# Attention decode with 32 heads: query projection, output projection and FFN weights moved into the head loop

## The chip, the cores and the metric

The kernel runs on one core of one Trainium2 chip. The metric is device time in microseconds (us) of one execution, as the median over several runs. The core has five engines with a queue each (PE for matmuls, DVE for vector work, ACT for activations and copies, POOL, and SP), and 16 DMA engines that all DMA queues feed. SP and ACT issue DMAs on a hardware queue each; POOL can issue DMAs too, which the kernel before does not do.

## The reference

One token goes through one transformer layer: a layer norm, attention of 32 heads over a cache of 32768 keys, a residual, a second layer norm, and a two-layer FFN with ReLU and a residual.

```
x: [1,1,640]   k_cache, v_cache: [1,32,32768,192]   wq: [640,6144]   wo: [6144,640]   w1: [640,1536]   w2: [1536,640]   (all bf16)

q  = (layernorm(x) @ wq) as 32 heads of 192
p  = softmax(q . k * 192**-0.5)           per head, over 32768 keys
o  = p . v                                per head
h  = x + concat(o) @ wo
out = h + relu(layernorm(h) @ w1) @ w2
```

The two caches are 805 MB together and are read once; all weights together are 20 MB.

## The kernel before

It has three stages.

**Start.** `x` is loaded and normalised on one partition. Ten short matmuls spread the result over 128 partitions (`LB`, line 95). The whole of `wq` comes in one DMA on SP's queue (line 97); 160 matmuls of 128x192 (line 101) make each head's query, already spread over all partitions, and 32 copies (line 103) leave them in `QB`.

**Head loop.** 32 heads of 8 chunks of 4096 keys, 256 chunks in all. For each chunk a K tile (SP's queue, line 120) and a V tile (ACT's queue, line 125) of 1536 KB each are loaded; both pools have three buffers. A tile holds 32 keys on each partition. For each of the 32, DVE multiplies 128x192 keys by the query and sums along the row into one column of the score tile `S` (line 133). Each such instruction shows in the trace as a pair: the product (`CUSTOM_DVE_ANT_0`) and a read of the accumulator into `S` (`DVE_READ_ACCUMULATOR2_ANT`). There are 8192 pairs. `S` is bf16 (line 14 and 129). ACT takes the exponential of `S` into `E` and its row sum into `ZP` (line 138); PE multiplies `E` with the V tile, 32 matmuls a chunk, summed in PSUM over the head (line 141); ACT copies the head's sum out (line 145).

**End.** The softmax sums are reduced and inverted (lines 151 to 155), each head's output is scaled and turned onto partitions by 64 products (lines 159 and 161), `wo` is loaded as `WOA` and `WOB` (lines 170 and 171), and 128 matmuls project it (lines 175 and 177, 64 of 512 columns, 64 of 128). Then come the residual (line 181), the second layer norm (lines 186 to 204), `W1` and `W2` (loaded on lines 212 and 214), and the FFN (lines 207 to 239).

The program's text sets the order of work only in part: the framework's scheduler places the instructions on each engine by their dependences and buffers, and adds the waits. Each engine takes its own list in order.

Of the kernel before, what the change touches and what calls it, by code (L numbers as in the profile page):

```python
# [7 lines left out]
F32 = mybir.dt.float32  # L8
BF16 = mybir.dt.bfloat16
ACT = mybir.ActivationFunctionType  # L10
ALU = mybir.AluOpType
AX = mybir.AxisListType

SCORE_BF16 = True


@with_exitstack
def kernel(
# [12 lines left out]
    nc = tc.nc  # L31
    P = nc.NUM_PARTITIONS

    _, _, D = A_x.shape
    _, H, Sk, Dh = A_k_cache.shape
    HD = H * Dh
    Dff = B_w1.shape[1]
    DC = D // P
    FC = Dff // P
    inv_sqrt_dh = Dh ** -0.5  # L40
    eps = 1e-5
    P64 = Dh - P

    CH = 4096 if Sk % 4096 == 0 else Sk
    assert Sk % CH == 0
    J = CH // P
    CN = Sk // CH

    persist = ctx.enter_context(tc.tile_pool(name="persist", bufs=1))
    ones11 = persist.tile([1, 1], F32)  # L50
# [3 lines left out]
    ones_col = persist.tile([P, 1], F32)  # L54
    nc.vector.memset(ones_col[:], 1.0)
    x32 = persist.tile([1, D], F32)
    QB = persist.tile([P, H, Dh], BF16)
    OUTR = persist.tile([1, H, Dh], F32)
    ZP = persist.tile([P, H, CN], F32)

    with (
        tc.tile_pool(name="pro_sb", bufs=1) as psb,
        tc.tile_pool(name="pro_sb2", bufs=2) as psb2,
        tc.tile_pool(name="pro_ps", bufs=1, space=bass.MemoryType.PSUM) as pps,
        tc.tile_pool(name="pro_ps2", bufs=2, space=bass.MemoryType.PSUM) as pps2,
    ):
        xbf = psb.tile([1, D], BF16)
        nc.sync.dma_start(out=xbf[:], in_=A_x[0])
        nc.vector.tensor_copy(out=x32[:], in_=xbf[:])
        msum = psb.tile([1, 1], F32)  # L70
        nc.vector.reduce_sum(out=msum[:], in_=x32[:], axis=AX.X)
        negmean = psb.tile([1, 1], F32)
        nc.vector.tensor_scalar_mul(out=negmean[:], in0=msum[:], scalar1=-1.0 / D)
        cen = psb.tile([1, D], F32)
        nc.vector.tensor_scalar_add(out=cen[:], in0=x32[:], scalar1=negmean[:, 0:1])
        junk_r = psb.tile([1, D], F32)
        var = psb.tile([1, 1], F32)
        nc.vector.tensor_tensor_reduce(
            out=junk_r[:], in0=cen[:], in1=cen[:], scale=1.0 / D, scalar=0.0,
            op0=ALU.mult, op1=ALU.add, accum_out=var[:],  # L80
        )
        vareps = psb.tile([1, 1], F32)
        nc.vector.tensor_scalar_add(out=vareps[:], in0=var[:], scalar1=eps)
        std = psb.tile([1, 1], F32)
        nc.scalar.activation(std[:], vareps[:], ACT.Sqrt)
        rstd = psb.tile([1, 1], F32)
        nc.vector.reciprocal(out=rstd[:], in_=std[:])
        ln32 = psb.tile([1, D], F32)
        nc.vector.tensor_scalar_mul(out=ln32[:], in0=cen[:], scalar1=rstd[:, 0:1])
        LB_ps = pps.tile([P, DC, P], F32)  # L90
        for c in range(DC):
            nc.tensor.matmul(LB_ps[:, c, :], lhsT=ln32[0:1, c * P:(c + 1) * P], rhs=ones_row[0:1, :],
                             start=True, stop=True)
        LB = psb.tile([P, DC, P], BF16)
        nc.vector.tensor_copy(out=LB[:], in_=LB_ps[:])
        WQ = psb.tile([P, DC, HD], BF16)
        nc.sync.dma_start(out=WQ[:], in_=A_wq.rearrange("(c p) n -> p c n", p=P))
        for h in range(H):
            qb_ps = pps2.tile([P, Dh], F32)
            for c in range(DC):  # L100
                nc.tensor.matmul(qb_ps[:], lhsT=LB[:, c, :], rhs=WQ[:, c, h * Dh:(h + 1) * Dh],  # L101
                                 start=(c == 0), stop=(c == DC - 1))
            nc.any.tensor_copy(out=QB[:, h, :], in_=qb_ps[:])  # L103

    k_h = A_k_cache[0]
    v_h = A_v_cache[0]

    with (
        tc.tile_pool(name="kpool", bufs=3) as kpool,
        tc.tile_pool(name="vpool", bufs=3) as vpool,  # L110
        tc.tile_pool(name="spool", bufs=2) as spool,
        tc.tile_pool(name="epool", bufs=2) as epool,
        tc.tile_pool(name="jpool", bufs=2) as jpool,
        tc.tile_pool(name="opsum", bufs=2, space=bass.MemoryType.PSUM) as opsum,
    ):
        for h in range(H):
            o_ps = opsum.tile([1, Dh], F32)
            for c in range(CN):
                Kt = kpool.tile([P, J, Dh], BF16)
                nc.sync.dma_start(  # L120
                    out=Kt[:],
                    in_=k_h[h, c * CH:(c + 1) * CH, :].rearrange("(p j) d -> p j d", p=P),
# [3 lines left out]
                    out=Vt[:],  # L126
                    in_=v_h[h, c * CH:(c + 1) * CH, :].rearrange("(p j) d -> p j d", p=P),
                )
                S = spool.tile([P, J], BF16 if SCORE_BF16 else F32)
                with nc.allow_low_precision(reason="scores tiny; bf16 accum enables DVE 2x mode"):  # L130
                    for j in range(J):
                        junk = jpool.tile([P, Dh], BF16)
                        nc.vector.tensor_tensor_reduce(  # L133
                            out=junk[:], in0=Kt[:, j, :], in1=QB[:, h, :], scale=inv_sqrt_dh,
                            scalar=0.0, op0=ALU.mult, op1=ALU.add, accum_out=S[:, j:j + 1],
                        )
                E = epool.tile([P, J], BF16)
                nc.scalar.activation(E[:], S[:], ACT.Exp, bias=0.0, scale=1.0,  # L138
                                     accum_out=ZP[:, h, c:c + 1])
                for j in range(J):  # L140
                    nc.tensor.matmul(  # L141
                        o_ps[0:1, :], lhsT=E[:, j:j + 1], rhs=Vt[:, j, :],
                        start=(c == 0 and j == 0), stop=(c == CN - 1 and j == J - 1),
                    )
            nc.scalar.copy(out=OUTR[0:1, h, :], in_=o_ps[0:1, :])  # L145

    esb = ctx.enter_context(tc.tile_pool(name="epi_sb", bufs=1))
    nblk = [(0, 0, 512), (1, 512, D - 512)]
    with tc.tile_pool(name="eps1", bufs=1, space=bass.MemoryType.PSUM) as eps1:
        ZH = esb.tile([P, H], F32)  # L150
        nc.vector.reduce_sum(out=ZH[:], in_=ZP[:], axis=AX.X)
        ZT_ps = eps1.tile([1, H], F32)
        nc.tensor.matmul(ZT_ps[:], lhsT=ones_col[:, 0:1], rhs=ZH[:, :], start=True, stop=True)
        RZ = esb.tile([1, H], F32)
        nc.vector.reciprocal(out=RZ[:], in_=ZT_ps[:])  # L155
        OCA_ps = eps1.tile([P, H], F32)
        OCB_ps = eps1.tile([P64, H], F32)
        for h in range(H):
            nc.tensor.matmul(OCA_ps[:, h:h + 1], lhsT=OUTR[0:1, h, 0:P], rhs=RZ[0:1, h:h + 1],  # L159
                             start=True, stop=True)  # L160
            nc.tensor.matmul(OCB_ps[:, h:h + 1], lhsT=OUTR[0:1, h, P:Dh], rhs=RZ[0:1, h:h + 1],  # L161
                             start=True, stop=True)
        OCA = esb.tile([P, H], BF16)
        OCB = esb.tile([P64, H], BF16)
        nc.vector.tensor_copy(out=OCA[:], in_=OCA_ps[:])  # L165
        nc.vector.tensor_copy(out=OCB[:], in_=OCB_ps[:])
        wo3 = A_wo.rearrange("(h r) n -> r h n", r=Dh)
        WOA = esb.tile([P, H, D], BF16)
        WOB = esb.tile([P64, H, D], BF16)
        nc.sync.dma_start(out=WOA[:], in_=wo3[0:P])  # L170
        nc.scalar.dma_start(out=WOB[:], in_=wo3[P:Dh])
        ATT_ps = eps1.tile([1, 2, 512], F32)
        for bi, c0, nw in nblk:
            for h in range(H):
                nc.tensor.matmul(ATT_ps[0:1, bi, 0:nw], lhsT=OCA[:, h:h + 1],  # L175
                                 rhs=WOA[:, h, c0:c0 + nw], start=(h == 0), stop=False)
                nc.tensor.matmul(ATT_ps[0:1, bi, 0:nw], lhsT=OCB[:, h:h + 1],  # L177
                                 rhs=WOB[:, h, c0:c0 + nw], start=False, stop=(h == H - 1))
        h32 = esb.tile([1, D], F32)
        for bi, c0, nw in nblk:  # L180
            nc.vector.tensor_tensor(out=h32[0:1, c0:c0 + nw], in0=x32[0:1, c0:c0 + nw],  # L181
                                    in1=ATT_ps[0:1, bi, 0:nw], op=ALU.add)

    with tc.tile_pool(name="eps2", bufs=1, space=bass.MemoryType.PSUM) as eps2:
        msum2 = esb.tile([1, 1], F32)
        nc.vector.reduce_sum(out=msum2[:], in_=h32[:], axis=AX.X)  # L186
# [8 lines left out]
            op0=ALU.mult, op1=ALU.add, accum_out=var2[:],  # L195
# [12 lines left out]
                             start=True, stop=True)  # L208
        lnT = esb.tile([P, DC], BF16)
        nc.vector.tensor_copy(out=lnT[:], in_=lnT_ps[:])  # L210
        W1 = esb.tile([P, DC, Dff], BF16)
        nc.sync.dma_start(out=W1[:], in_=B_w1.rearrange("(c p) n -> p c n", p=P))
        W2 = esb.tile([P, FC, D], BF16)
        nc.scalar.dma_start(out=W2[:], in_=B_w2.rearrange("(c p) n -> p c n", p=P))
        nff = Dff // 512
        H1_ps = eps2.tile([1, nff, 512], F32)
        H1r = esb.tile([1, Dff], F32)
# [54 lines left out]
```

## Time and profile before

| | us |
|---|---|
| median of 4 runs (2447.7 to 2450.02) | 2449.45 |
| the profiled execution | 2450.02 |
| its span in the trace | 2448.2 |
| start, to the first score instruction | 49.43 |
| head loop on DVE | 2288.14 |
| end, after the last score instruction | 110.63 |

The profiled execution took 1.8 us more than its span. The table's lower half splits the span at two instructions of DVE: the first and the end of the last of line 133. DVE is busy for 94% of the span, PE for 55%, ACT for 4%. Busy time counts neither waiting nor the issue of DMAs.

### The profile page before, as it was taken

How to read it: one execution, taken by the hardware profiler on the slowest of the kernel's cores; microseconds unless marked ns; L12 is line 12 of the kernel's file. 1: busy time of each engine (PE TensorE's matmuls, PEld its weight loads, DVE VectorE, ACT ScalarE, POOL GpSimd, SP SyncE). 2: the span in 40 equal slices, each digit the busy share in tenths (PEclk: the TensorE clock that was granted, in tenths of full speed). 3: DMA queues.
4: the chain of work that ended last, by engine and by line, in shares of the span. 5: the costliest groups of instructions: out<-in, count | busy, mean ns of one | idle time of the engine just before them, and what ended most of it. 6: DMA issues, size and time to landing. Idle time of an engine off the chain costs nothing. (4 is left out here: it accounts for less than half of the span.)

```text
span 2448.2 us, 35960 instructions
## 1 busy us (share of the span) xinstructions
PE 1339.8 (55%) x8693; PEld 1003.6 (41%) x8693; DVE 2301.2 (94%) x16419; ACT 105.7 (4%) x580; POOL 0.2 (0%) x4
## 2 busy tenths in 40 slices
PE   3555555555555555555555555555555555555578
PEld 3444444344444443444444444443444444444452
DVE  2999999999999999999999999999999999999921
ACT  2000000000000000000000000000000000000000
POOL 0000000000000000000000000000000000000000
PEclk8666666666666666666666666666666666666655
DMA  6889888889888889888889888889888889888860
GB/s 271 350 358 364 353 348 352 340 356 368 351 352 352 341 352 371 349 352 351 340 352 370 353 353 352 342 349 372 353 348 344 351 352 369 348 356 340 346 193 1
DMA packets 82984, 827.30 MB, mean 338 GB/s; under 512 B 8274, under 2 KB 15956, under 8 KB 16596
## 3 DMA queue, kind: packets, MB, share of 16 engines
q1 hardware_dynamic: 42292, 417.75, 43.9%
q10 hardware_dynamic: 40480, 407.26, 41.1%
q8 instruction: 68, 1.11, 0.2%
q14 instruction: 144, 1.18, 0.1%
HBM read 824.97 MB, written 0.00 MB: 337 GB/s over the span
## 5 line engine op out<-in xcount | busy, mean ns | idle before, releaser
L133 DVE CUSTOM_DVE_ANT_0 junk<-Kt,QB 128x192 bf16<-128x192 bf16 x8192 | 2287.5, 355 | 10.4 <-DMA Kt<-in_A_k_cache_dram 9.9
L141 PE MATMUL o_ps<-Vt,E 128*1 128x192 bf16 x8192 | 1231.9, 342 | 1072.1 <-ACT E L138 1072.1
L141 PEld LDWEIGHTS <-E 128*1 128x1 bf16 x8192 | 943.2, 118 | 1360.8 <-ACT E L138 1145.9
L133 DVE DVE_READ_ACCUMULATOR2_ANT S<- 128x1 bf16 x8192 | 709.5, 87 | 0.0
L138 ACT ACTIVATE E<-S 128x32 bf16<-128x32 bf16 x256 | 58.5, 228 | 2093.6 <-DVE S L133 2093.6
L181 DVE TENSOR_TENSOR h<-x,ATT_ps 1x512 f32<-1x512 f32 (+1 forms) x2 | 1.0, 476 | 52.3 <-PE ATT_ps L177 52.3
L138 ACT ACTIVATION_READ_ACCUMULATOR E<-S 128x1 f32 x256 | 47.7, 186 | 0.2
L175 PE MATMUL ATT_ps<-WOA,OCA 128*1 128x512 bf16 (+1 forms) x64 | 27.3, 427 | 7.9 <-DMA WOA<-in_A_wo_dram 7.9
L103 DVE CAST QB<-qb_ps 128x192 bf16<-128x192 f32 x1 | 0.4, 357 | 29.5 <-PE qb_ps L101 29.5
L177 PE MATMUL ATT_ps<-WOB,OCB 64*1 64x512 bf16 (+1 forms) x64 | 26.9, 420 | 0.0
L101 PE MATMUL qb_ps<-WQ,LB 128*128 128x192 bf16 x160 | 17.0, 259 | 13.3 <-DMA WQ<-in_A_wq_dram 13.3
L165 DVE CAST OCA<-OCA_ps 128x32 bf16<-128x32 f32 x1 | 0.2, 191 | 24.8 <-PE OCA_ps L159 24.8
L101 PEld LDWEIGHTS <-LB 128*128 128x128 bf16 x160 | 14.7, 103 | 15.7 <-issue 12.3
L159 PE MATMUL OCA_ps<-RZ,OUTR 1*128 1x1 f32 x64 | 17.8, 345 | 0.4 <-DVE RZ L155 0.4
L159 PEld LDWEIGHTS OCA_ps<-RZ,OUTR 1*128 1x128 f32 x64 | 15.1, 292 | 1.0 <-DVE RZ L155 0.6
L177 PEld LDWEIGHTS <-OCB 64*1 64x1 bf16 x64 | 4.9, 76 | 25.6 <-issue 21.9
L145 ACT COPY OUTR<-o_ps 1x192 f32<-1x192 f32 x32 | 9.7, 304 | 116.2 <-PE o_ps L141 116.2
L175 PEld LDWEIGHTS <-OCA 128*1 128x1 bf16 x64 | 5.1, 79 | 17.5 <-issue 13.9
L161 PE MATMUL OCB_ps<-RZ,OUTR 1*64 1x1 f32 x64 | 11.6, 247 | 0.0
L103 ACT CAST QB<-qb_ps 128x192 bf16<-128x192 f32 x31 | 9.9, 318 | 23.5 <-PE qb_ps L101 22.2
L161 PEld LDWEIGHTS OCB_ps<-RZ,OUTR 1*64 1x64 f32 x64 | 8.8, 195 | 0.5
L223 DVE TENSOR_SCALAR H1r<-H_ps 1x512 f32<-1x512 f32 x3 | 2.0, 679 | 5.0 <-PE H_ps L220 5.0
(48 smaller groups left out, 47.3 us busy)
## 6 DMA issues: line engine op xcount, KB each, us to landing
Kt<-in_A_k_cache_dram SPq DMA_DIRECT2D x256, 1536.0 KB, 9.2
Vt<-in_A_v_cache_dram ACTq DMA_DIRECT2D x256, 1536.0 KB, 9.8
WQ<-in_A_wq_dram SPq DMA_DIRECT2D x1, 7680.0 KB, 21.0
WOA<-in_A_wo_dram SPq DMA_DIRECT2D x1, 5120.0 KB, 34.0
WOB<-in_A_wo_dram ACTq DMA_DIRECT2D x1, 2560.0 KB, 26.2
W<-in_B_w_dram SPq DMA_DIRECT2D x1, 1920.0 KB, 40.0
W<-in_B_w_dram ACTq DMA_DIRECT2D x1, 1920.0 KB, 37.9
xbf<-in_A_x_dram SPq DMA_DIRECT2D x1, 1.2 KB
```

The costliest lines, as they stand in the source:

```text
L101: nc.tensor.matmul(qb_ps[:], lhsT=LB[:, c, :], rhs=WQ[:, c, h * Dh:(h + 1) * Dh], start=(c == 0), stop=(c == DC - 1))
L103: nc.any.tensor_copy(out=QB[:, h, :], in_=qb_ps[:])
L133: nc.vector.tensor_tensor_reduce(out=junk[:], in0=Kt[:, j, :], in1=QB[:, h, :], scale=inv_sqrt_dh, scalar=0.0, op0=ALU.mult, op1=ALU.add, ...
L138: nc.scalar.activation(E[:], S[:], ACT.Exp, bias=0.0, scale=1.0, accum_out=ZP[:, h, c:c + 1])
L141: nc.tensor.matmul(o_ps[0:1, :], lhsT=E[:, j:j + 1], rhs=Vt[:, j, :], start=(c == 0 and j == 0), stop=(c == CN - 1 and j == J - 1),)
L145: nc.scalar.copy(out=OUTR[0:1, h, :], in_=o_ps[0:1, :])
L159: nc.tensor.matmul(OCA_ps[:, h:h + 1], lhsT=OUTR[0:1, h, 0:P], rhs=RZ[0:1, h:h + 1], start=True, stop=True)
L161: nc.tensor.matmul(OCB_ps[:, h:h + 1], lhsT=OUTR[0:1, h, P:Dh], rhs=RZ[0:1, h:h + 1], start=True, stop=True)
L175: nc.tensor.matmul(ATT_ps[0:1, bi, 0:nw], lhsT=OCA[:, h:h + 1], rhs=WOA[:, h, c0:c0 + nw], start=(h == 0), stop=False)
L177: nc.tensor.matmul(ATT_ps[0:1, bi, 0:nw], lhsT=OCB[:, h:h + 1], rhs=WOB[:, h, c0:c0 + nw], start=False, stop=(h == H - 1))
L181: nc.vector.tensor_tensor(out=h32[0:1, c0:c0 + nw], in0=x32[0:1, c0:c0 + nw], in1=ATT_ps[0:1, bi, 0:nw], op=ALU.add)
L223: nc.vector.tensor_relu(out=H1r[0:1, nb * 512:(nb + 1) * 512], in_=H1_ps[0:1, nb, :])
```

## The change

What it does:

- `wq` is no longer loaded whole. Heads 0 to 3 have a piece each in `WQF`, loaded at the start; later heads load a piece `WQh` (two buffers) in the loop. These DMAs are on POOL's queue. Each head's query is made in the loop by five matmuls, and copied by ACT into `QBh` (two buffers).
- `wo` is loaded in 16 pieces `WOp` on POOL's queue: four at the start, one for every second head. A one-element copy on POOL ahead of a piece makes it wait for an earlier head's row sum.
- Each head's tail runs within the next head's first chunk or two: ACT copies its output, DVE reduces its row sums (`ZHh`) and inverts the total (`RZh`), PE scales and turns the output (`AUX`) and adds four matmuls of the projection to `ATT_ps`, which is summed in PSUM over all heads.
- `W1` and `W2` are loaded on POOL's queue at head 26.
- `S` is float32 instead of bf16.

```
-                S = spool.tile([P, J], BF16 if SCORE_BF16 else F32)
+                S = spool.tile([P, J], F32)
...
-        WQ = psb.tile([P, DC, HD], BF16)
-        nc.sync.dma_start(out=WQ[:], in_=A_wq.rearrange("(c p) n -> p c n", p=P))
-        for h in range(H):
-            qb_ps = pps2.tile([P, Dh], F32)
...
+    NF = 4
+    WQF = persist.tile([P, NF, DC, Dh], BF16)
+    for hh in range(NF):
+        nc.gpsimd.dma_start(
+            out=WQF[:, hh],
+            in_=A_wq[:, hh * Dh:(hh + 1) * Dh].rearrange("(c p) n -> p c n", p=P),
+        )
+    WOp = [persist.tile([P, 3, D], BF16, name=f"WOp{i}") for i in range(HC // 3)]
+    wo_v = A_wo.rearrange("(c p) n -> p c n", p=P)
+    def load_wo(i):
+        nc.gpsimd.dma_start(out=WOp[i][:], in_=wo_v[:, 3 * i:3 * i + 3, :])
+    for i in range(3):
+        load_wo(i)
...
+        def head_tail_1(h, o_ps):
+            ORh = hpool.tile([1, Dh], F32, tag="ORh")
+            nc.scalar.copy(out=ORh[:], in_=o_ps[0:1, :])
+            ZHh = hpool.tile([P, 1], F32, tag="ZHh")
+            nc.vector.reduce_sum(out=ZHh[:], in_=ZP[:, h, :], axis=AX.X)
+            zt_ps = ztps.tile([1, 1], F32)
+            nc.tensor.matmul(zt_ps[:], lhsT=ones_col[:, 0:1], rhs=ZHh[:, 0:1], start=True, stop=True)
+            return ORh, zt_ps
+        def head_tail_2(h, ORh, zt_ps):
+            RZh = hpool.tile([1, 1], F32, tag="RZh")
+            nc.vector.reciprocal(out=RZh[:], in_=zt_ps[:])
...
+            nc.tensor.matmul(AUX[pA:P, colA:colA + 1], lhsT=ORh[0:1, 0:lenA], rhs=RZh[0:1, 0:1],
+                             start=True, stop=True)
+            nc.scalar.copy(out=OCh[pA:P, 0:1], in_=AUX[pA:P, colA:colA + 1])
...
+            for bi, c0, nw in nblk:
+                nc.tensor.matmul(ATT_ps[0:1, bi, 0:nw], lhsT=OCh[pA:P, 0:1],
+                                 rhs=WOp[h // 2][pA:P, cA % 3, c0:c0 + nw], start=first_att[bi], stop=lastA)
...
         for h in range(H):
+            if h < NF:
+                WQh = WQF[:, h]
+            else:
+                WQh = wqpool.tile([P, DC, Dh], BF16)
+                nc.gpsimd.dma_start(
+                    out=WQh[:],
+                    in_=A_wq[:, h * Dh:(h + 1) * Dh].rearrange("(c p) n -> p c n", p=P),
+                )
+            qb_ps = qbps.tile([P, Dh], F32)
+            for c in range(DC):
+                nc.tensor.matmul(qb_ps[:], lhsT=LB[:, c, :], rhs=WQh[:, c, :],
+                                 start=(c == 0), stop=(c == DC - 1))
+            QBh = qbpool.tile([P, Dh], BF16)
+            nc.scalar.copy(out=QBh[:], in_=qb_ps[:])
+            if h % 2 == 0 and h // 2 + 3 < HC // 3:
+                i = h // 2 + 3
+                if h > 0:
+                    nc.gpsimd.tensor_copy(out=WOp[i][0:1, 0, 0:1], in_=ZP[0:1, h - 1, 0:1])
+                load_wo(i)
+            if h == H - 6:
+                for Wt in (W1, W2):
+                    nc.gpsimd.tensor_copy(out=Wt[0:1, 0, 0:1], in_=ZP[0:1, h - 1, 0:1])
+                nc.gpsimd.dma_start(out=W1[:], in_=B_w1.rearrange("(c p) n -> p c n", p=P))
+                nc.gpsimd.dma_start(out=W2[:], in_=B_w2.rearrange("(c p) n -> p c n", p=P))
...
                 for j in range(J):
+                    if c == 0 and j == 4 and pend is not None:
+                        mid = head_tail_1(*pend)
+                    if c == 0 and j == 26 and pend is not None:
+                        head_tail_2(pend[0], *mid)
                     junk = jpool.tile([P, Dh], BF16)
```

Three places where instructions move. The first is the start of the DMA queues. On SP before, `wq` stood ahead of the K tiles:

```order
L68 DMA xbf<-in_A_x_dram 1x640
L97 DMA WQ<-in_A_wq_dram 128x5x6144
L120 DMA Kt<-in_A_k_cache_dram 128x6144 x256
L170 DMA WOA<-in_A_wo_dram 128x32x640
L212 DMA W_27041<-in_B_w_dram 128x5x1536
```

Now SP has `x` and then the K tiles alone, and POOL's queue begins with the pieces of the weights:

```order
L101 DMA WQF<-in_A_wq_dram 128x5x192 x4
L109 DMA WOp_108<-in_A_wo_dram 128x3x640
L109 DMA WOp_109<-in_A_wo_dram 128x3x640
L109 DMA WOp_110<-in_A_wo_dram 128x3x640
L109 DMA WOp_111<-in_A_wo_dram 128x3x640
L173 DMA WQh<-in_A_wq_dram 128x5x192 x2
L187 CAST WOp_112<-ZP 1x1
L109 DMA WOp_112<-in_A_wo_dram 128x3x640
```

What moved: the first K tile's DMA no longer stands behind the load of `wq`.

The second is DVE at the turn from the first head to the second. Before, the pairs of the next head (`S_1187`) follow the last of the head before (`S_1082`) with nothing between:

```order
L133 ISA junk_1145,S_1082<-Kt_1078,QB_65 128x192
L133 ISA S_1082 128x1
L133 ISA junk_1188,S_1187<-Kt_1183,QB_65 128x192
L133 ISA S_1187 128x1
L133 ISA junk_1190,S_1187<-Kt_1183,QB_65 128x192
L133 ISA S_1187 128x1
```

Now the row sum of the head before stands behind the fourth pair of the next head:

```order
L213 ISA junk_1022,S_1015<-Kt_1011,QBh_1008 128x192
L213 ISA S_1015 128x1
L137 TENSOR_REDUCE ZHh_1026<-ZP_65 128x1
L213 ISA junk_1030,S_1015<-Kt_1011,QBh_1008 128x192
L213 ISA S_1015 128x1
```

What moved: a reduction comes between two pairs, and 22 pairs later, in the same manner, `L144 RECIPROCAL RZh_1074<-zt_ps_1028 1x1`, which waits for PE. For 19 of the 31 heads with a successor the two stand behind pairs 4 and 26 of the next head, for nine behind pairs 19 and 36, and for three between these.

The third is PE at the same turn. Before, it has only matmuls of V tiles there:

```order
L141 LDWEIGHTS E_1147
L141 MATMUL o_ps_356<-Vt_1080,E_1147 1x192
L141 LDWEIGHTS E_1252
L141 MATMUL o_ps_1182<-Vt_1185,E_1252 1x192
L141 LDWEIGHTS E_1252
```

Now, after the last matmul of the first head (`o_ps_177`), the total of its row sums, a later head's query (five matmuls, one shown), the turn of its output and its projection:

```order
L221 MATMUL o_ps_177<-Vt_901,E_968 1x192
L139 MATMUL zt_ps_1028<-ZHh_1026,ones_col_62 1x1
L179 MATMUL qb_ps_2704<-WQF_103,LB_66 128x192
L151 MATMUL AUX_167<-RZh_1074,ORh_1024 128x1
L155 MATMUL AUX_167<-RZh_1074,ORh_1024 64x1
L160 MATMUL ATT_ps_130<-WOp0_108,OCh_1076 1x512
L164 MATMUL ATT_ps_130<-WOp0_108,OCh_1076 1x512
L160 MATMUL ATT_ps_130<-WOp0_108,OCh_1076 1x128
L164 MATMUL ATT_ps_130<-WOp0_108,OCh_1076 1x128
L221 LDWEIGHTS E_1097
```

What moved: the total that DVE's reciprocal waits for stands behind all V matmuls of the head, and the query made here is that of the head after the next two.

## Rows read from the trace of the kernel before

**Rows 1.** The page: busy time by engine.
```profile
PE 1339.8 (55%) x8693; PEld 1003.6 (41%) x8693; DVE 2301.2 (94%) x16419; ACT 105.7 (4%) x580; POOL 0.2 (0%) x4
```
**Rows 2.** Windows: stretch, length, busy us (instructions) by engine, PE clock, DMA share, GB/s.
```profile
0.00:49.43 49.43, 19.49 (x170) 16.91 (x170) 5.04 (x15) 12.63 (x34) 0.20 (x4) 0.93 0.57 236
49.43:2337.57 2288.14, 1226.82 (x8160) 939.29 (x8160) 2287.65 (x16384) 90.92 (x541) 0.00 (x0) 0.69 0.88 351
...
2422.93:2448.20 25.27, 17.91 (x73) 9.45 (x73) 6.47 (x15) 0.20 (x1) 0.00 (x0) 0.63 0.00 1
```
**Rows 3.** Waits of DVE within the loop: total us, times, longest.
```profile
DVE junk L133 <- issue: 0.4, 2, 0.2
```
**Rows 4.** Groups by form: busy us, mean ns, idle before.
```profile
L133 DVE CUSTOM_DVE_ANT_0 junk<-Kt,QB 128x192 bf16<-128x192 bf16 x8192 | 2287.5, 355 | 10.4 <-DMA Kt<-in_A_k_cache_dram 9.9 <-issue 0.4
L133 DVE DVE_READ_ACCUMULATOR2_ANT S<- 128x1 bf16 x8192 | 709.5, 87 | 0.0
...
L78 DVE CUSTOM_DVE_ANT_0 junk_r<-cen 1x640 f32<-1x640 f32 x1 | 0.8, 811 | 0.0
L71 DVE TENSOR_REDUCE msum<-x 1x1 f32<-1x640 f32 x1 | 0.8, 807 | 0.0
...
L151 DVE TENSOR_REDUCE ZH<-ZP 128x32 f32<-128x256 f32 x1 | 0.4, 420 | 5.7 <-issue 5.7
...
L87 DVE RECIPROCAL rstd<-std 1x1 f32<-1x1 f32 x1 | 0.2, 151 | 0.3 <-ACT std L85 0.3
...
L78 DVE DVE_READ_ACCUMULATOR2_ANT var<- 1x1 f32 x1 | 0.1, 70 | 0.0
```
**Rows 5.** Timeline of the start: begin, length, instruction.
```profile
1.13 0.40 SPq L97 DMA_DIRECT2D WQ<-in_A_wq_dram  x1
...
8.87 0.83 DVE L95 CAST LB<-LB_ps 128x640 bf16<-128x640 f32 x1 [2.59 <-PE LB_ps L92]
...
22.13 17.00 PE L101 MATMUL qb_ps<-WQ,LB 128*128 128x192 bf16 x160 [13.30 <-DMA WQ<-in_A_wq_dram]
...
23.12 0.32 ACT L103 CAST QB<-qb_ps 128x192 bf16<-128x192 f32 x1 [17.61 <-PE qb_ps L101]
...
39.20 28.54 SPq L120 DMA_DIRECT2D Kt<-in_A_k_cache_dram  x5
...
49.43 0.36 DVE L133 CUSTOM_DVE_ANT_0 junk<-Kt,QB 128x192 bf16<-128x192 bf16 x1 [9.91 <-DMA Kt<-in_A_k_cache_dram]
```
**Rows 6.** Windows with the fastest and a slow stretch of the DMAs.
```profile
46.00:50.00 4.00, 0.00 (x0) 0.00 (x0) 0.57 (x5) 0.00 (x0) 0.00 (x0) 0.50 1.04 442
...
2352.00:2357.00 5.00, 5.00 (x27) 4.82 (x26) 0.00 (x0) 1.28 (x1) 0.00 (x0) 0.50 1.09 267
```
**Rows 7.** Line 120: K tiles from issue to landing.
```profile
DMA to landing us min/median/max: 7.9/9.2/24.0
```
**Rows 8.** Timeline of the end.
```profile
2337.68 0.23 ACT L138 ACTIVATE E<-S 128x32 bf16<-128x32 bf16 x1 [8.63 <-DVE S L133]
...
2338.05 5.10 PE L141 MATMUL o_ps<-Vt,E 128*1 128x192 bf16 x32 [4.50 <-ACT E L138]
2343.19 0.31 ACT L145 COPY OUTR<-o_ps 1x192 f32<-1x192 f32 x1 [5.19 <-PE o_ps L141]
...
2343.77 0.22 PE L153 MATMUL ZT_ps<-ZH,ones_col 128*1 128x32 f32 x2 [0.61 <-ACT OUTR L145]
...
2347.37 0.58 PE L159 MATMUL OCA_ps<-RZ,OUTR 1*128 1x1 f32 x2
```
**Rows 9.** The chain that ended last: begin, length, what.
```profile
2343.23 34.02 DMA WOA<-in_A_wo_dram
...
2377.88 0.51 PE ATT_ps L177
...
2422.20 0.20 PE ATT_ps L175
...
2422.62 0.29 DVE h L181
```

## Prediction: the time of the changed kernel

> **What bounds the kernel now.** I read the busy line first: DVE at 94%, PE at 55% [rows 1]. A share over the whole span says little, so the windows come next. They cut the span into a start of 49.43 us, a loop of 2288.14 us in which DVE is busy for 2287.65, and an end of 110.63 us of which the last 25.27 are the second norm and the FFN [rows 2]. The waits confirm the loop: DVE waits there for 0.4 us in all, and for no DMA [rows 3]. So the loop is DVE's pace, 2288.14 / 8192 = 279.3 ns a pair, and what PE, ACT and the DMAs save there is worth nothing. The start and the end are the opposite: DVE stands, and a chain of DMA and PE work sets the time. In the timeline of the start, `wq` is issued at 1.13, its 160 matmuls begin only at 22.13 and take 17.00, and only then is the first K tile issued, at 39.20, which DVE meets at 49.43 [rows 5]. In the end, the chain goes through 34.02 us of `WOA` and then through the 128 projection matmuls until 2422.6 [rows 9]. Start and end hold 160 us without a score.
>
> **The start.** `wq` leaves SP's queue, so the first K tile is issued where `wq` was, at 1.13. Before, it took 49.43 - 39.20 = 10.23 us from issue to DVE's first pair [rows 5]; the same gives 11.4. The other condition is the first query. `LB` ends at 9.70, unchanged; before, the first five matmuls and the start of the copy came 23.12 - 22.13 = 0.99 later, and the copy takes 0.32 [rows 5]: 11.0, if `WQF`'s first piece has landed. New beside the K and V tiles is POOL's queue, with six pieces of `wq` of 0.246 MB and four of `wo` of 0.492 MB, 3.44 MB in all. The trace has no DMA of POOL. From below, it costs nothing: 11.4. From above, POOL's bytes and the first three K and three V tiles, 9.44 MB, all land before the first query's piece: 12.9 MB at 442 GB/s [rows 6] is 29.1, with the issue at 1.1 and 1.3 for matmuls and copy 31.6. I take 13.0, near the lower end, because the first piece is 0.246 MB and first in its queue, and at that rate takes 0.6 us by itself, 1.7 with three queues sharing; the 1.6 over 11.4 is a K tile that shares with a third queue which moves less than the other two. The gain is 49.4 - 13.0 = 36.4. The later tiles of the first 60 us get part of the same load: 3.44 MB is 7.8 us of DMA at full rate, against a margin of a fifth (442 GB/s possible, 351 used [rows 2, 6]). I add nothing for it.
>
> **The pairs with a float32 `S`.** The product's length is 355 ns for 192 bf16 elements and 811 for 640 float32 elements [rows 4]: (811 - 355) / (640 - 192) = 1.02 ns an element for both types. So the bf16 pair has no faster pace per element that float32 could lose. The accumulator read takes 87 ns on 128 partitions to bf16, and 70 on one to float32 [rows 4]. Bounds for the pair: nothing, as the slope says, or 17 ns less, if the whole difference of the reads showed in the pace. I take nothing; the slope is measured on the instruction that carries the work.
> The Trainium skill, page "VectorE: DVE Perf Modes", section "What auto-detection actually checks", has a rule against this edit: two elements a cycle need every tensor to be of 16 bits, and a float32 output would take that away. The row gives one element per 1.02 ns already, so the trace speaks against the rule's having an effect here. By the row the edit costs 0 us; by the rule it would be the second rival.
>
> **What the loop gains in work on DVE.** 31 of the 32 heads put a reduction of 8 elements and a reciprocal of 1 between pairs. The reduction: 420 ns for 256 elements, 807 for 640, so 1.01 an element and 420 - 248 x 1.01 = 170 for 8; the reciprocal: 151 [rows 4]. A product's record is 355 long and the next begins after 279, so 76 ns of neighbours overlap. If both new ones overlap so, a head costs 321 - 152 = 169 ns, 5.2 us in all; if they do not and each also breaks one overlap of the pairs, with 40 ns for each wait, 553 ns, 17.1 us. I take their plain lengths, 321 ns: 10.0 us.
>
> **New waits on DVE.** Behind a waiting DVE instruction all later pairs stand, so this is where the loop could lose most. The reduction waits for the exponential of the last chunk: in the end that begins 0.11 after the last pair (2337.57) and is over with its accumulator by 2338.05 [rows 8], 0.5 us, while the reduction comes at the earliest after four pairs, 1.1 us. The reciprocal waits for the total on PE, which stands behind the head's last 32 matmuls. They end at 2343.15, 5.6 us after the last pair, and the total takes 0.22 [rows 8]: 5.9 us. The reciprocal comes after 26 pairs at the earliest, 7.3 us. Both waits end early, the second by 1.4 us. The queries are made a head or more ahead of their use, so the first pair of a head waits only for K as before.
>
> **PE, ACT, DMAs in the loop.** Per head PE gets five query matmuls (17.00 / 32 = 0.53 us), the total, two turns (0.58 at the most each [rows 8]) and four projections (two of 0.51 and two of 0.20 [rows 9]), some 3.3 us in 71.5; it is idle for 46% of the loop [rows 2]. ACT gets four copies of about 0.3 us. Where a copy stands ahead of an exponential, PE starts that chunk a microsecond or two late and still ends before the next. The DMAs take 7.9 MB of `wq`, 7.9 of `wo`, 3.9 of `W1` and `W2`. Even at the slow 267 GB/s [rows 6] that is 74 us against 12% idle of 2288, 275 us [rows 2]. A K tile lands 9.2 us after its issue [rows 7] and is used two chunks, 17.9 us, after it. Hidden, then; if the cover went at one transfer, the largest, `W1` and `W2` together, could hold one tile for 14.7 us and cost 6.
>
> **The end.** From the last pair the matmuls end after 5.58, then in a row: the total 0.22, the reciprocal 0.15, the first turn 0.58, a copy 0.31, the second turn 0.37 to 0.58, four projections 1.42, with some 0.04 between each, and the second residual 0.31 to the start of the norm [rows 4, 8, 9]: 9.2. The rest stays at 25.27 [rows 2]: 34.5. `WOA` and 124 of the projection matmuls are out of it. From below: PE is busy for 17.9 of the 25.27 at a clock of 0.63; at full clock 6.6 less, 28. From above: 3 more for a table load that loses its cover, and for waits of the new short chain, 37.5.
>
> **The sum.** 13.0 + 2288.1 + 10.0 + 34.5 = 2345.6 of span, and 1.8 around it as in the profiled execution: 2347. That execution stood 0.6 above the median, which I leave. The terms' bounds give 11.4 + 2288.1 + 5.2 + 28 + 1.8 = 2335 and 31.6 + 2288.1 + 17.1 + 37.5 + 1.8 = 2376.
>
> **The rivals.**
> First, a late query: POOL's queue gets its turn only when K and V have filled their buffers. For it: two queues alone fill all 16 engines while the buffers fill, a DMA share of 1.04 [rows 6]; against it, that the piece is small. The 10.23 us of the first K tile are 7.1 for 3.15 MB of K and V at 442 GB/s and 3.1 besides. So 1.1 + 3.1 + 21.4 for 9.44 MB + 1.3 put the first pair at 27, and the time at 2361.
> Second, the slower side: the float32 `S` slows the pair. For it: the comment on line 130 claims a doubled mode for bf16; against it, the slope above. The price is 8192 times whatever a pair gains, and it decides at 101 / 8.192 = 12.3 ns. Half of 192 x 1.02 ns, what a lost doubling would cost, is 98 ns: 802 us, 3149.
> Third, the opposite: the read to float32 is shorter, by up to 17 ns a pair, 139 us: 2208. For it the two rows; against it that they differ in partitions too.
> Fourth, DVE loses time to POOL. 50 DMAs and 14 one-element copies are new on an engine that did nothing. No row shows what that does to DVE. If DVE stood for as long as SP takes to issue one DMA, 0.40 us [rows 5], it is 20 us: 2367; it would take 2 us each to eat the gain.
> The Trainium skill, page "SBUF — State Buffer", section "Who interferes with whom", says that a vector instruction with two SBUF inputs contends with a GpSimd instruction that reads SBUF, and not with one that only writes it. By that the 14 copies could each hold one pair of 0.36 us, 5 us in all, which would make it 2352. No run here shows it.
>
> **How the numbers follow.** Forecast 0.69, with its own range from 2335 to 2360; late query 0.11; slower pairs 0.05; shorter reads 0.05; POOL's hold 0.10, of which 0.01 cancels the gain. The range of 2333 to 2378 takes in the bounds and the first and fourth rival, and leaves out the second and third. Within 0.2% (5 us, about what a measurement of this kernel tells from no change) lies only that 0.01: faster 0.94, same 0.01, slower 0.05.
>
> **What would show it.** DVE's first pair at 12 to 14 us confirms the start, at 25 or later the first rival. The pair's pace at 279 ns over the loop decides the second and third. Idle time of DVE before `ZHh` and `RZh` should be near zero; more than 1 us a head means that the total on PE comes later than I worked out. The last pair to the end of the span should be near 34.5, without a DMA in the chain but that of the result. A K tile that DVE waits for would mean that the new DMAs are not hidden. The prediction is wrong if DVE's loop is longer than 2320 or the start later than 32.

## The result, and the profile after

The changed kernel takes 2341.7 us (median of 8 runs, 2338.64 to 2343.58) against 2447.75 us before (13 runs beside them): a ratio of 0.9562, 95% interval 0.9553 to 0.9572. The profiled execution took 2342.4 us with a span of 2340.6, which is 107.6 us less than the span before.

The busy line of the changed kernel, to be held against [rows 1]:

```profile
PE 1324.2 (57%) x8755; PEld 994.1 (42%) x8755; DVE 2304.2 (98%) x16478; ACT 111.4 (5%) x645; POOL 673.6 (29%) x68
```

DVE's busy time has hardly changed, 2304.2 against 2301.2 us; its share rose from 94% to 98% because the span shrank around it. New is POOL, busy for 673.6 us with 68 instructions. The windows, cut at the first and the end of the last pair as in [rows 2] (length, then busy us by engine, PE clock, DMA share, GB/s):

```profile
0.00:15.07 15.07, 3.46 (x15) 2.86 (x15) 4.88 (x14) 1.80 (x3) 7.90 (x13) 1.00 0.88 338
15.07:2306.91 2291.84, 1296.69 (x8625) 976.83 (x8625) 2291.70 (x16446) 107.18 (x635) 665.74 (x55) 0.70 0.90 359
2306.91:2340.60 33.69, 24.01 (x115) 14.42 (x115) 7.65 (x19) 2.44 (x7) 0.00 (x0) 0.65 0.00 1
```

The start gave 34.4 us (49.43 to 15.07), the end 76.9 (110.63 to 33.69), and the loop took back 3.7 (2288.14 to 2291.84): 107.6 together. Two of DVE's waits over the whole span, for the first K tile and at the reciprocal of a head's tail (total us, times, longest), beside [rows 3]:

```profile
DVE junk L213 <- DMA Kt<-in_A_k_cache_dram: 5.3, 1, 5.3
DVE RZh L144 <- PE zt_ps L139: 5.2, 1, 5.2
```

Both happened once, the first ahead of the first pair, the second after the last. Between 20 and 2300 us DVE waits for nothing at all: neither the 31 reciprocals nor any K tile held it. The groups by form (busy us, mean ns, idle before), beside [rows 4]:

```profile
L213 DVE CUSTOM_DVE_ANT_0 junk<-Kt,QBh 128x192 bf16<-128x192 bf16 x8192 | 2290.8, 343 | 5.4 <-DMA Kt<-in_A_k_cache_dram 5.3
...
L213 DVE DVE_READ_ACCUMULATOR2_ANT S<- 128x1 f32 x8192 | 587.2, 72 | 0.0
L187 POOL CAST WOp<-ZP 1x1 bf16<-1x1 f32 x12 | 491.7, 40979 | 567.3 <-ACT E L218 481.5 <-ACT OCh L157 85.8
L191 POOL CAST W<-ZP 1x1 bf16<-1x1 f32 x2 | 139.0, 69522 | 2.2 <-ACT OCh L157 2.2
...
L144 DVE RECIPROCAL RZh<-zt_ps 1x1 f32<-1x1 f32 x32 | 4.8, 151 | 5.2 <-PE zt_ps L139 5.2
L137 DVE TENSOR_REDUCE ZHh<-ZP 128x1 f32<-128x8 f32 x32 | 4.7, 147 | 0.5 <-ACT E L218 0.5
```

The records of the product and of the read are shorter than before (343 and 72 ns against 355 and 87), and yet pairs with nothing between them begin every 279.2 ns, against 279.3 before. A record's length is not its price here. The same rows show what nobody had in the sum: a copy of one element on POOL takes 41 us on average. The timeline of the start (begin, length, instruction), beside [rows 5]:

```profile
0.74 0.86 ACTq L202 DMA_DIRECT2D Vt<-in_A_v_cache_dram  x2
...
1.13 1.73 SPq L197 DMA_DIRECT2D Kt<-in_A_k_cache_dram  x3
...
12.30 0.96 PE L179 MATMUL qb_ps<-WQF,LB 128*128 128x192 bf16 x5 [3.43 <-DMA WQF<-in_A_wq_dram]
...
13.30 0.32 ACT L182 CAST QBh<-qb_ps 128x192 bf16<-128x192 f32 x1 [7.74 <-PE qb_ps L179]
...
15.07 0.36 DVE L213 CUSTOM_DVE_ANT_0 junk<-Kt,QBh 128x192 bf16<-128x192 bf16 x1 [5.34 <-DMA Kt<-in_A_k_cache_dram]
```

The first query is there at 13.62 and the K tile at 15.0, 13.9 after its issue instead of 10.2. Two V tiles were issued 0.39 us ahead of it. The query was late too: its piece of `wq`, 0.246 MB, landed 11.0 us after its issue, and PE stood for it for 3.43 us.

What held the first K tile in the kernel before was not the order of SP's queue alone. SP's own waits there name the query matmuls (total us, times, longest):

```profile
SPq L120 <- PE qb_ps L101: 29.4, 1, 29.4
```

The text of the kernel before closes the pool that holds `WQ` (line 62) before it opens that of the K tiles (line 109); the changed kernel has no `WQ`. That the K tiles took over the space of `WQ`, and so had to wait for its last matmul, is inferred from this; no run takes it apart from the queue's order.

A place in the loop shows POOL's copy beside DVE (same columns, the turn to the fifth head):

```profile
239.64 66.67 POOL L187 CAST WOp<-ZP 1x1 bf16<-1x1 f32 x1 [3.08 <-ACT E L218]
...
305.92 0.34 DVE L213 CUSTOM_DVE_ANT_0 junk<-Kt,QBh 128x192 bf16<-128x192 bf16 x1
306.20 0.07 DVE L213 DVE_READ_ACCUMULATOR2_ANT S<- 128x1 f32 x1
306.20 0.14 DVE L137 TENSOR_REDUCE ZHh<-ZP 128x1 f32<-128x8 f32 x1
306.27 0.34 DVE L213 CUSTOM_DVE_ANT_0 junk<-Kt,QBh 128x192 bf16<-128x192 bf16 x1
306.55 0.07 DVE L213 DVE_READ_ACCUMULATOR2_ANT S<- 128x1 f32 x1
```

Two things are to be seen. Without the reduction the next product would have begun at 306.20; it begins at 306.27. So the reduction, whose record is 140 ns long, costs DVE 70. And the copy on POOL, begun at 239.64, ends at 306.31, just when DVE for once runs something other than a pair. The end, beside [rows 8] and [rows 9]:

```profile
2307.32 5.28 PE L221 MATMUL o_ps<-Vt,E 128*1 128x192 bf16 x32 [4.18 <-ACT E L218]
...
2312.40 0.23 PE L139 MATMUL zt_ps<-ZHh,ones_col 128*1 128x1 f32 x2
...
2314.19 0.43 PE L164 MATMUL ATT_ps<-WOp,OCh 128*1 128x512 bf16 x2
...
2315.51 0.81 DVE L235 TENSOR_REDUCE msum<-h 1x1 f32<-1x640 f32 x1
```

From the last pair to the start of the second norm are 8.6 us, where 34 us of `WOA` and 128 matmuls stood.

### The profile page after: what moved, and what is told of

Its sections match the earlier page's. It is cut to its first block, busy times and chain, and to the rows that moved or that the text cites. A ratio compares the mean times of both kernels' runs of the same rounds, so it can differ in the third digit from the quotient of the medians.

```text
span 2340.6 us, 36341 instructions
## 1 busy us (share of the span) xinstructions
PE 1324.2 (57%) x8755; PEld 994.1 (42%) x8755; DVE 2304.2 (98%) x16478; ACT 111.4 (5%) x645; POOL 673.6 (29%) x68
## 5 line engine op out<-in xcount | busy, mean ns | idle before, releaser
L213 DVE CUSTOM_DVE_ANT_0 junk<-Kt,QBh 128x192 bf16<-128x192 bf16 x8192 | 2290.8, 343 | 5.4 <-DMA Kt<-in_A_k_cache_dram 5.3
L187 POOL CAST WOp<-ZP 1x1 bf16<-1x1 f32 x12 | 491.7, 40979 | 567.3 <-ACT E L218 481.5
L213 DVE DVE_READ_ACCUMULATOR2_ANT S<- 128x1 f32 x8192 | 587.2, 72 | 0.0
L173 POOL DMA_DIRECT2D WQh<-in_A_wq_dram x28 | 24.6, 878 | 718.2 <-PE qb_ps L179 442.6
L218 ACT ACTIVATE E<-S 128x32 bf16<-128x32 f32 x256 | 58.6, 229 | 1969.8 <-DVE S L213 1969.8
L191 POOL CAST W<-ZP 1x1 bf16<-1x1 f32 x2 | 139.0, 69522 | 2.2 <-ACT OCh L157 2.2
L164 PE MATMUL ATT_ps<-WOp,OCh 64*1 64x512 bf16 (+1 forms) x64 | 19.7, 393 | 7.1 <-ACT OCh L157 7.1
L160 PE MATMUL ATT_ps<-WOp,OCh 128*1 128x512 bf16 (+1 forms) x64 | 17.6, 354 | 0.0
L179 PE MATMUL qb_ps<-WQh,LB 128*128 128x192 bf16 x140 | 17.4, 258 | 0.0
L109 POOL DMA_DIRECT2D WOp<-in_A_wo_dram x16 | 12.7, 796 | 3.6 <-POOL WOp L187 3.6
## 6 DMA issues: line engine op xcount, KB each, us to landing
WQF<-in_A_wq_dram POOLq DMA_DIRECT2D x4, 240.0 KB, 17.2
```

The lines of the kernel that those rows point to most:

```text
L109: nc.gpsimd.dma_start(out=WOp[i][:], in_=wo_v[:, 3 * i:3 * i + 3, :])
L160: nc.tensor.matmul(ATT_ps[0:1, bi, 0:nw], lhsT=OCh[pA:P, 0:1], rhs=WOp[h // 2][pA:P, cA % 3, c0:c0 + nw], start=first_att[bi], stop=lastA)
L164: nc.tensor.matmul(ATT_ps[0:1, bi, 0:nw], lhsT=OCh[0:lenB, 1:2], rhs=WOp[h // 2][0:lenB, cA % 3 + 1, c0:c0 + nw], start=False, stop=lastB)
L173: nc.gpsimd.dma_start(out=WQh[:], in_=A_wq[:, h * Dh:(h + 1) * Dh].rearrange("(c p) n -> p c n", p=P),)
L179: nc.tensor.matmul(qb_ps[:], lhsT=LB[:, c, :], rhs=WQh[:, c, :], start=(c == 0), stop=(c == DC - 1))
L187: nc.gpsimd.tensor_copy(out=WOp[i][0:1, 0, 0:1], in_=ZP[0:1, h - 1, 0:1])
```

## The experiments

The theory is the prediction's sum: the start and the end each lose a serial piece, DVE's pairs keep their pace, and the new work hides behind them. Its rivals are those of the prediction. All ratios are to runs of the kernel before on the same chip. `tail_x8`, `recip_early`, `all_at_start`, `pool_probe` and `fold_floor` are one execution each and are read by their traces more than by their times.

**Each half undone.** In `old_end` the heads' tails and the weights of the end go back behind the loop:

```
-        head_tail_1 / head_tail_2 and load_wo, W1, W2 in the loop
+            nc.scalar.copy(out=OUTR[0:1, h, :], in_=o_ps[0:1, :])
+    (after the loop: sums, turns, WOA/WOB, 128 projection matmuls, W1, W2 as before)
```

> The changed kernel's start and loop with the end of the kernel before: no head tails in the loop, wo, W1 and W2 loaded after the loop. Theory (start and end are separate, the loop is DVE's): the end is 110.6 again, the loop loses its reductions and reciprocals (3.7), so 2342 + 76.9 - 3.7 = 2415. Rival (the loop paid for the loads hidden in it, or the end's gain needs the new start): more than 8 us away from that.

2413.54 us, ratio 0.9854 [0.9837, 0.987]. Its start takes 14.96 us; the windows of its loop and its end:

```profile
14.96:2303.16 2288.20, 1243.62 (x8315) 948.73 (x8315) 2287.70 (x16384) 98.88 (x573) 22.62 (x26) 0.70 0.89 354
2303.16:2412.00 108.84, 93.00 (x363) 47.10 (x363) 8.56 (x22) 2.12 (x5) 0.00 (x0) 0.55 0.35 109
```

As expected: the end is worth 75 us, and without the tails the loop is back at its old length.

In `old_start` the whole `wq` and all the queries go back ahead of the loop, while POOL's pieces of `wo` stay:

```
-            five query matmuls per head, WQF / WQh on POOL's queue
+        nc.sync.dma_start(out=WQ[:], in_=A_wq.rearrange("(c p) n -> p c n", p=P))
+        for h in range(H): ... QB[:, h, :]
```

> The changed kernel's loop and end with the start of the kernel before: wq whole on SP's queue, all 32 queries made before the first K tile. Theory: the first pair is at 49 to 50 us again instead of 15.1, all else unchanged: 2342 + 34.4 = 2376. Rival as for the old end: more than 8 us away.

2382.11 us, ratio 0.9726 [0.9712, 0.9741], 6 us above the expectation and within the 8 that it allowed. The timeline of its start shows why:

```profile
27.53 17.08 PE L105 MATMUL qb_ps<-WQ,LB 128*128 128x192 bf16 x160 [18.83 <-DMA WQ<-in_A_wq_dram]
```

The 160 matmuls begin at 27.53 instead of 22.13 [rows 5], since `wq` now shares the DMAs with four pieces of `wo` (1.97 MB): up to those matmuls the DMAs moved 357 GB/s on average, against 355 before, and so needed 5.4 us longer for the larger load. K is issued at 44.68 and the first pair begins at 55.02.

**The type of `S` alone** (`s_bf16`):

```
-                S = spool.tile([P, J], F32)
+                S = spool.tile([P, J], BF16)
```

> The changed kernel with S back in bf16 and nothing else. Theory: the pair's pace does not depend on the type of S, so 2342 within 0.2%, with 279.1 ns a pair in both; the read of the accumulator goes back from 72 to 87 ns in its record without moving the pace. Rival: some of the gain is the float32 read, 15 ns shorter in its record; then the loop grows by up to 8192 x 15 ns, 123 us, to 2465.

2342.61 us, ratio 0.9565 [0.955, 0.9579], with the same loop of 2291.85 us. The pair's records:

```profile
L214 DVE CUSTOM_DVE_ANT_0 junk<-Kt,QBh 128x192 bf16<-128x192 bf16 x8192 | 2290.8, 342 | 5.3 <-DMA Kt<-in_A_k_cache_dram 5.3
L214 DVE DVE_READ_ACCUMULATOR2_ANT S<- 128x1 bf16 x8192 | 610.7, 75 | 0.0
```

The type costs nothing, which ends the second and the third rival. It does not explain the shorter records either: with bf16 the read is at 75 ns, not at the 87 of before. What shortened them stays open.

**What a small DVE operation costs between pairs** (`tail_x8`):

```
+            for _ in range(8):
+                nc.vector.reduce_sum(out=XT[:], in_=ZP[:, h, :], axis=AX.X)
```

> The changed kernel with eight more reductions of 8 elements at each head's turn, 248 in the loop. Theory from the trace after (a reduction sets the next pair back by 70 ns, half its record): the loop grows by 17 us to 2309. Rival (the plain length of 144 to 170 ns, as the forecast took it): by 36 to 42 us.

2356.28 us. The loop is 2309.94 us long, 18.1 more, for 248 reductions: 73 ns each. The timeline has them 70 ns apart, though each record is 150 long:

```profile
88.60 0.16 DVE L138 TENSOR_REDUCE ZHh<-ZP 128x1 f32<-128x8 f32 x1
88.67 0.15 DVE L140 TENSOR_REDUCE XT<-ZP 128x1 f32<-128x8 f32 x1
88.74 0.35 DVE L216 CUSTOM_DVE_ANT_0 junk<-Kt,QBh 128x192 bf16<-128x192 bf16 x1
```

**The wait that the prediction says is hidden, uncovered** (`recip_early`):

```
-                    if c == 0 and j == 26 and pend is not None:
+                    if c == 0 and j == 8 and pend is not None:
```

> The changed kernel with the reciprocal asked for behind pair 8 instead of 26; the scheduler puts it behind pairs 14 or 15 for 8 of 31 heads and at 25 or later for the rest. Theory (the wait is hidden only because 26 pairs, 7.3 us, stand ahead of it, and the total on PE is ready 5.9 us after the head's last pair): DVE waits about 1.6 us at each of the 8, 13 us in all, and none at the others. Rival (the total is ready much earlier, the place is free): no wait.

2350.83 us, with DVE's waits in the loop:

```profile
DVE RZh L144 <- PE zt_ps L139: 11.2, 8, 1.9
```

The loop is 2303.43 us long, 11.6 more. So the total on PE does end some 6 us after a head's last pair, and it is the place of the reciprocal that hides it.

**The weights' DMAs, uncovered** (`all_at_start`):

```
-    a piece of wo for every second head, W1 and W2 at head 26, each behind a POOL copy
+    all 16 pieces, W1 and W2 issued on POOL's queue at the start, no copies
```

> The changed kernel with all 16 pieces of wo, W1 and W2 issued on POOL's queue at the start, and no one-element copies on POOL. Theory (the DMAs can move 440 GB/s and the loop uses 351, but a third queue takes its share first come): in the first 60 us DVE waits for K tiles, 5 to 20 us in all, and then never. Rival (the margin of a fifth covers any load): no wait beyond the first tile. Both expect the loop's pace without POOL's copies unchanged at 279.1 ns.

2361.32 us: slower than the changed kernel by 20, by another way than expected. DVE's waits between 100 and 200 us, and PE's:

```profile
DVE junk L205 <- ACT E L210: 13.3, 1, 13.3
DVE junk L205 <- DMA Kt<-in_A_k_cache_dram: 5.1, 5, 1.5
...
PE qb_ps L181 <- DMA WQh<-in_A_wq_dram: 25.9, 1, 25.9
```

K tiles were late by 5.1 us, at the low end of what was expected, but between 100 and 200 us and not in the first 60. The larger loss is a later head's query. Its piece of `wq` was issued at 104.79, behind all of `wo`, `W1` and `W2` (11.8 MB), and PE has it at 193.87. Its five matmuls stand on PE ahead of V's. PE stands for 25.9 us; with it wait the exponentials, whose `E` buffers PE has not freed, and then DVE, which has no `S` to write. The pairs without POOL's copies beside them keep the changed kernel's pace, 279.2 ns, as theory and rival both expected.

**POOL beside DVE** (`pool_probe`, in the middle of four heads):

```
+                    nc.gpsimd.memset(SC[:], 0.0)
+                    nc.gpsimd.tensor_copy(out=SD[:], in_=ZP[0:1, h, 3:4])
```

> The changed kernel with two more one-element operations on POOL in four heads, in the middle of a head where DVE runs pairs only: a memset, which only writes, and a copy that reads SBUF. Theory (a POOL instruction that reads SBUF cannot start while DVE runs products with two SBUF inputs back to back, and one that only writes can): the memset takes about 0.1 us, the copy tens of us, until DVE's next reduction or another gap; DVE's pace stays at 279.1 ns. Rival (POOL's long copies are a matter of the copy's own start or of the trace): both take alike, or the copy ends at once.

2342.74 us, the loop unchanged at 2291.8. POOL's timeline in two of the four heads:

```profile
750.17 0.09 POOL L220 MEMSET SC<- 1x1 f32 x1 [11.70 <-ACT SC L219]
767.57 26.98 POOL L223 COPY SD<-ZP 1x1 f32<-1x1 f32 x1 [17.31 <-ACT E L225]
...
1036.43 0.09 POOL L220 MEMSET SC<- 1x1 f32 x1 [0.85 <-ACT SC L219]
1054.01 40.66 POOL L223 COPY SD<-ZP 1x1 f32<-1x1 f32 x1 [17.49 <-ACT E L225]
```

Writing takes POOL 0.09 us, reading 27 to 41 us, and DVE loses nothing to either. The Trainium skill, page "SBUF — State Buffer", section "Who interferes with whom", says that a two-input DVE instruction contends with a GpSimd instruction that reads and not with one that only writes. The trace agrees on who contends. On the size it goes further: the copy waits not for one pair of 0.28 us, but for as many as 239 in a row (66.67 us, in the changed kernel's row above); the longest, ahead of `W2`, took 75.84 us there.

**Why the first K tile is late.** The first guess was POOL's load at the start (`lean_start`):

```
+            if h == 0:
+                nc.scalar.copy(out=WOp[i][0:1, 0, 0:1], in_=QBh[0:1, 0:1])   (same for WQF 1 to 3)
+                load_wo(i)
```

> The changed kernel with heads 1 to 3 of wq and the first four pieces of wo held back until the first query is made, by a one-element copy on ACT into each. Theory (the first K tile landed late, at 15.0, because 3 MB on POOL's queue shared the engines): K lands by 12.5, the first pair is at 12.0 to 13.0, the time 2 to 3 us lower, 2339. Rival (the K tile is late for another reason, or the held pieces hit the second tile): the first pair stays at 15, or the gain is lost in a wait for a later tile.

2339.81 us, ratio 0.9557 [0.9543, 0.9571]; the first pair at 15.13. The guess fell. The second was the V tiles (`v_held`):

```
                 Vt = vpool.tile([P, J, Dh], BF16)
+                if h == 0 and c < 2:
+                    nc.scalar.copy(out=Vt[0:1, 0, 0:1], in_=QBh[0:1, 0:1])
```

> The first two V tiles are held back until the first query is made (a one-element copy by ACT writes into each tile ahead of its load). Theory: the first K tile lands late because the V tiles, issued 0.39 us ahead of it, take half of the DMAs' rate: about 5 MB had moved in the changed kernel when the first pair began at 15.07, against 3.7 MB in the kernel before. Without V, K's tile and the first pieces land well before 13, and the first query, ready at 13.6 in the changed kernel, sets the start, or sooner if its own piece lands sooner: first pair between 11 and 13.7, time 1.4 to 4 us below the changed kernel's. Rival: the tile is late because the DMAs start up slowly, whoever asks; then the first pair stays at 15.0 and the time the same. V is used first at 24, so that its later loads cost nothing on either theory.

2354.43 us, ratio 0.9607 [0.9594, 0.962]: the start does what the theory says, and the time still goes up by 13. The first row is DVE at the start; the others are POOL, PE and ACT at 1950:

```profile
11.15 0.36 DVE L215 CUSTOM_DVE_ANT_0 junk<-Kt,QBh 128x192 bf16<-128x192 bf16 x1 [1.42 <-ACT QBh L182]
...
1879.45 67.47 POOL L191 CAST W<-ZP 1x1 bf16<-1x1 f32 x1
1946.86 0.88 POOL L192 DMA_DIRECT2D W<-in_B_w_dram  x1
1947.73 1.04 POOL L193 DMA_DIRECT2D W<-in_B_w_dram  x1
1948.77 1.73 POOL L173 DMA_DIRECT2D WQh<-in_A_wq_dram  x2
...
1978.41 0.98 PE L179 MATMUL qb_ps<-WQh,LB 128*128 128x192 bf16 x5 [27.31 <-DMA WQh<-in_A_wq_dram]
...
1979.94 0.16 ACT L153 CAST OCh<-AUX 128x1 bf16<-128x1 f32 x1 [28.52 <-PE AUX L151]
```

The first pair comes 3.92 us earlier, so the V tiles are what delayed K, and the first query's piece with it: its matmuls begin at 9.79 instead of 12.30 and no longer wait for a DMA. That the 0.39 us of lead makes the difference to the kernel before is not shown: K took 10.2 us there and 10.3 in `old_start`, where V was issued together with it, but no run changes the lead alone. The loop is 17.2 us longer (2309.04). 16.6 of it is one wait of DVE for `E`. The edit changed the scheduler's lists: one more piece of `wq` now stands on POOL behind the two long copies and behind `W1` and `W2`. It lands 27 us after PE wants it. The changed kernel runs the same two copies (138.99 us from 1815 on), but the piece for the query made there was issued ahead of them, at 1812, and PE does not wait.

**A version with less DVE work** (`fold`): 32 pairs a chunk become one product over the whole tile, three halvings in place and one sum.

```
+                nc.vector.tensor_tensor(out=prod[:], in0=Kt[:], in1=<query for all 32 keys>, op=ALU.mult)
+                while w > 24:
+                    w //= 2
+                    nc.vector.tensor_tensor(out=prod[:, :, 0:w], in0=prod[:, :, 0:w], in1=prod[:, :, w:2 * w], op=ALU.add)
+                nc.vector.reduce_sum(out=S[:], in_=prod[:, :, 0:w], axis=AX.X)
```

> The changed kernel with the 32 pairs of a chunk replaced by five DVE instructions: one bf16 product of the whole K tile with the query, three halvings of it in place by bf16 adds of 96, 48 and 24 columns, and one sum of the last 24 to float32. Theory (a pair is 200 ns of elements at one a cycle and 79 ns besides; the product and the adds run at two a cycle): 3.2 + 1.6 + 0.8 + 0.4 + 0.8 = 6.8 us and some 0.4 for five instructions, 7.2 us a chunk against 8.93; the DMAs need 7.1 at 442 GB/s; a loop of 1850 to 1950 and a time of 1900 to 2000. Rival (two inputs from SBUF run at one element a cycle here as in the pair): 6.4 + 3.2 + 1.6 + 0.8 + 0.8 = 12.8 us a chunk, a loop of 3280.

2055.32 us, ratio 0.8396 [0.8382, 0.841]: faster than both kernels, slower than expected. DVE's groups:

```profile
L208 DVE TENSOR_TENSOR prod<-Kt,QBh 128x6144 bf16<-128x6144 bf16 x256 | 859.7, 3358 | 16.8 <-DMA Kt<-in_A_k_cache_dram 8.3
L214 DVE TENSOR_TENSOR prod<-prod 128x3072 bf16<-128x3072 bf16 x256 | 449.9, 1758 | 7.6
L214 DVE TENSOR_TENSOR prod<-prod 128x1536 bf16<-128x1536 bf16 x256 | 245.0, 957 | 8.1
L215 DVE TENSOR_REDUCE S<-prod 128x32 f32<-128x768 bf16 x256 | 244.0, 953 | 22.8 <-DVE prod L214 0.9
L214 DVE TENSOR_TENSOR prod<-prod 128x768 bf16<-128x768 bf16 x256 | 142.7, 557 | 8.9
```

The product takes 3358 / 6144 = 0.55 ns an element, where the pair took 1.02 [rows 4]. A chunk's work is 7.58 us instead of 8.94, and with the gaps between the operations a chunk takes 7.8. The Trainium skill, page "VectorE: DVE Perf Modes", section "Side-by-side: where the cycles go for N=2048 bf16", gives two elements a cycle to 16-bit data; this product agrees, with 0.55 ns against the pair's 1.02, and the pair does not reach it. The expectation was missed at the small terms: it allowed 0.4 us for five instructions, but each took 0.15 to 0.16 us more than its elements were priced at, 0.78 in all, and the gaps between them took 0.25.

Two runs ask what comes next: `fold_v` holds V back as above, `fold_floor` also leaves out two of the three halvings.

```
-                while w > 24:
+                (only the halving to 96; the sum takes the first 24)
```

> The whole-tile product and three halvings (as in the run called fold, 2055.3), with V held back at the start as in the run beside it. Theory, that DVE's 7.58 us of work a chunk plus small gaps sets the pace: the start gains 1.4 to 4 us, the loop stays, 2051 to 2054. Rival, that the DMAs set the pace, with V's bytes only moved to later: the gain is given back and the time stays at 2055.

> As the run beside it, without the second and third halving (of the 96 partial sums of each key only 24 are summed), which takes 1.51 us a chunk off DVE. It asks what bounds the folded loop besides DVE. If DVE alone sets the pace, a chunk takes 6.2 us and the time is about 1650. If the DMAs set it, 805 MB at 410 to 442 GB/s, the best rates that the profiles so far show, take 1821 to 1964 us, and the time is 1870 to 2010, with DVE waiting for K in nearly every chunk. PE's 4.6 us a chunk at the clock of 0.74 would be hidden in either.

`fold_v`: 2055.89 us, ratio 0.8395 [0.8384, 0.8407]. The first pass of DVE begins at 11.16 instead of 15.32, and the 4 us are given back, as the rival said, but not in waits for K. Between 20 and 2020 us DVE's waits for K fall from 2.7 us in `fold` to 0.4, and those of the reciprocals for the total on PE rise from 3.2 to 10.5. PE's waits for V tiles rise from 48.3 to 78.3. `fold_floor`: 1996.39 us. Its loop from 20 to 1960, and DVE's two largest waits:

```profile
20.00:1960.00 1940.00, 1154.28 (x8587) 923.86 (x8587) 1545.83 (x826) 103.61 (x632) 57.65 (x54) 0.74 1.01 422
```

```profile
DVE prod L210 <- DMA Kt<-in_A_k_cache_dram: 229.0, 176, 3.4
DVE RZh L144 <- PE zt_ps L139: 132.0, 30, 8.9
```

387 us less DVE work brought 59: the DMAs are full at 422 GB/s, and DVE waits for K in 176 of the 256 chunks, not in nearly every one. It also waits 30 times for the total on PE, and PE itself waits 785 us for V tiles. The folded loop stands close to that second bound.

## Why the prediction held, and which terms were off

- **The whole.** Forecast 2347, measured 2341.7. The steps were right: a chain of DMA and PE work left the start and the end, and DVE's pace stayed. `old_start` and `old_end` each give back their part alone. The span came out 5.0 us below the sum's 2345.6, and that is less than its largest miss: the start took 2.1 us more than forecast, the loop 6.3 less and the end 0.8 less, so misses of opposite sign partly cancelled.
- **The pairs.** Priced at nothing, measured at nothing; `s_bf16` shows it for the type, and the second and third rival are refuted with it.
- **DVE's extra work: the term that was mis-sized.** The step took plain record lengths, 321 ns a head and 10.0 us; its low bound, with 76 ns of overlap for each operation, was 5.2. The low bound's reading was the right one. At the 31 turns of the trace after, a reduction (record 147 ns) sets the next pair back by 73 ns and a reciprocal (151) by 80, so 74 and 71 ns overlap; `tail_x8` shows the 73 again. That is 4.7 us, under the bound because the reduction had been taken at 170 ns. The pairs themselves gave back some 1.1 us, and the loop grew by 3.7. The 40 ns for each wait in the upper bound show nowhere. What counts in the pace is when the next instruction begins, not a record's length.
- **The start.** 13.0 forecast, 15.07 measured: inside its bounds, but later than the 12 to 14 that were to confirm the step. That K could be issued at 1.13 was right, but the step leaned on the queue alone and left out SP's wait for the query matmuls, which went with `WQ`. The 1.6 us over 11.4 were put down to a third queue, POOL's. `lean_start` shows that queue to be innocent. `v_held` shows the cause, the V tiles: before, K and V were issued together at 39.20, and now two V tiles go ahead of K. The first rival, a late query, was right in part. The piece of 0.246 MB, taken at 1.7 us at most, landed after 11.0; the query was ready at 13.62, 2.6 us later than worked out and still 1.4 before K, so it did not decide.
- **The new waits.** Hidden, as forecast. `recip_early` shows the 5.9 us of the total on PE and that its place hides them.
- **The DMAs.** Hidden, but the price of lost cover was too low. The step took a late K tile, 6 us. What came, in `v_held` and `all_at_start`, was a late piece of a query, at 16.6 and 13.3 us, because PE takes its list in order. The prediction's sentence that queries are made a head ahead is true of the matmuls, and said nothing of when their piece lands. That the changed kernel pays nothing for it was in part luck: the piece that `v_held` waits for was issued at 1812, 3 us ahead of POOL's two long copies.
- **The end.** 34.5 forecast, 33.69 measured.
- **POOL, the fourth rival.** The contention is real and has the other sign: POOL waits for DVE. The estimate by the Trainium skill's rule, 5 us of held pairs, is refuted with it.

## What to carry to other kernels

Where one engine's pace sets a long loop, take serial work at the ends into the loop, and price a small operation there by when the next one begins, not by its record. Then look at what a queue's order hides: a small transfer behind large ones, or behind an engine that stands, becomes a wait elsewhere, and an edit at the other end of the program can move it there. And when everything else is hidden, the gain left is in the loop's own instruction: the fold was worth 286 us, the whole change 106.

## What the runs showed of the hardware

A one-element copy on POOL that reads SBUF took up to 75.84 us while DVE ran its two-input pairs back to back, and a write of one element 0.09 us; DVE's pace was untouched. Of the changed kernel's 14 copies nine ended as DVE ran a reduction, and four of these had run on past a reciprocal. The other five ended among pairs alone, after 0.18 to 35.85 us, as did one in `pool_probe` at 794.55. What lets a copy in there stays open. With DVE on long products and halvings (`fold`) POOL was busy for 80.3 us in all instead of 673.6: no copy took more than 2.95 us, and 13 of the 14 ended within 0.05 us of the end of a whole-tile product.
